# Half-width weight blocks, a later feed forward and loads on another queue in attention with a gated feed forward

## The chip, the cores and the metric

The kernel runs on one core of a Trainium2 chip. The core has TensorE (matrix products, called PE in the profile; its weight loads are PEld), VectorE (DVE), ScalarE (ACT), GpSimd (POOL) and SyncE (SP, which only issues transfers), and 16 DMA engines that all issuing queues share. The metric is the device time of one execution in microseconds.

## The reference

Eight batches of eight heads attend causally over 576 tokens with 64 columns a head, with a bias that falls with the running sum of `s`; the result, 4608 tokens by 512, goes through a gated feed forward of 1536 hidden columns.

```python
scores = scale * np.matmul(q, k.transpose(0, 1, 3, 2))
cum = np.cumsum(np.maximum(s, 0.0), axis=-1)
bias = -(cum[:, :, :, None] - cum[:, :, None, :])
scores = np.where(causal, -1000000000.0, scores + np.minimum(bias, 0.0))
attn = softmax(scores)                       # the largest score is subtracted first
x = concat_heads(np.matmul(attn, v))         # 4608 x 512
out = (sigmoid(x @ w_gate) * (x @ w_val)) @ w_out
```

Inputs are float32.

## The kernel before

**Precision.** Except for the first eight heads, which are computed in float32 (names with `n_`), operands are split into a high and a low float16 part, and a product is made of three: high by high, high by low, low by high.

**Tiles of a head.** The 576 queries of a head are five tiles: tile 0 has 64 rows, tiles 1 to 4 have 128. Tile t sees 64 + 128 t keys. Scores come from TensorE (`s_part`, lines 423 and 424); GpSimd masks the bias row (`mask_part`, 438); VectorE adds the bias and takes the extreme (`max_part`, 448); ScalarE takes the exponential into a float32 tile `e` (451). `p_part` then makes the float16 weights of several tiles at once, as `SETS` groups them: tiles 0 to 2 (768 columns) and tiles 3 and 4 (1152 columns). ScalarE writes the high part (455), VectorE the low part (456), and one DMA transpose on SP's queue (459) turns both into blocks of 128 keys by 128 queries, tile `pt`. A tile of 64 + 128 t keys is padded to t + 1 blocks, its last block half zeros; so a head has 15 high and 15 low blocks. `av_part` multiplies each of the 15 blocks of keys three times with the values (lines 471 to 473, tile `av`), and `x_part` divides by the sum of the weights, which is one more column of v.

**Values.** `load_v` (397 to 402) loads v for a pair of heads, `split_v` (409 to 412) splits it into `v16`. The power of two by which v is scaled is one for a batch: `v_square` (line 152) loads all v of the batch in four pieces of 288 KB into tiles `vsq`, through GpSimd's queue, into buffers that the bias rows `rl` use too (two of them); `v_square_sum` (160) squares and adds them on ScalarE; `v_scale` (164 on) adds over partitions. It is done one batch ahead: load at t = 2, square at t = 4 of heads 1 to 4 of the batch before.

**Keys and queries.** `split_qk` splits and transposes them into `T`; `swap_k` copies the halves of `T` crosswise (`T<-T`, lines 383 and 384). From head 18 on (`EARLY`), `more_room` gives the space of `t2big`, which only the feed forward of the first two token groups needs, to more buffers (`spare`; `t2f` in the profile).

**The bias row.** `load_crow` fetches a row of `cum_d` (389); `spread_crow` broadcasts it over the partitions on GpSimd (392).

**Feed forward.** Tokens are 18 groups of 256. A unit is a group and a block of 128 of the 1536 hidden columns: `ffn_in` (24 matmuls, line 619; 48 where a group lies across two batches), a tanh on ScalarE (624), VectorE (626), a split (634, 635), and `ffn_out`, which follows some units later (649), and after the last block ScalarE's `osb` (656) and the store on GpSimd's queue (657). The operand x sits in ten slots `xslots` (`x_of`), four to a batch, filled through a DMA transpose (`x<-x`, 491).

**What sets the order.** One loop over ticks n writes everything out; head i and tile 4 - t of it have tick n = 5 i + t. `p_part` of head a comes at ticks 5 a + 3 and 5 a + 6, `av_part` of head i - 2 at t = 1 of head i. A batch's feed forward is spread over the 40 ticks of the next batch, `m` ticks behind. From this order of writing as priority, the framework works out, with modelled durations, the order on each engine's queue, which is then fixed; `tc.high_priority` moves work ahead, `tc.keep_in_program_order` (`pin`, from head 18 on) keeps an instruction at its place in the written order. On the chip each queue runs strictly in its order.

Of the kernel before, what the change touches and what calls it, by code (L numbers as in the profile page):

```python
# [7 lines left out]
F16 = mybir.dt.float16  # L8
F32 = mybir.dt.float32
# [3 lines left out]
AF = mybir.ActivationFunctionType  # L13
# [3 lines left out]
P = 128  # L17
# [6 lines left out]
def tile_attention_then_gated_ffn(  # L24
# [27 lines left out]
    PAD = NTL * P - S  # L52
    NN = H
    LAG = 3

# [17 lines left out]
    e_s = [cp.tile([P, n * P], F32, name=f"e_{i}") for i, (_, _, n) in enumerate(SETS)]  # L73
    p_s = [cp.tile([P, 2, n * P], F16, name=f"p16_{i}") for i, (_, _, n) in enumerate(SETS)]
    e_t, pf_t = {}, {}
    for i, (ts, first_block, n) in enumerate(SETS):
        for t, kb in zip(ts, first_block):
            cols = slice(kb * P, (kb + t + 1) * P)
            e_t[t] = e_s[i][:, cols]
            pf_t[t] = p_s[i].rearrange("p l n -> p (l n)").bitcast(F32)[:, cols]  # L80
    for t, (q0, m, w) in enumerate(TILES):
        nc.gpsimd.memset(e_t[t][:, w:], 0.0)
# [28 lines left out]
    def pin(ins):  # L111

        return tc.keep_in_program_order(ins) if spare else ins
# [34 lines left out]
    def v_square(b, c):  # L148
        if c == 0:
            vss[b] = wp.tile([P, vch], F32, tag="vss", name=f"vss{b}")  # L150
        t = wp.tile([P, S], F32, tag="rl", name=f"vsq{b}_{c}")
        nc.gpsimd.dma_start(t, vview[b, c])
        if b == 0:
            nc.scalar.activation(t, t, AF.Square, accum_out=vss[b][:, c : c + 1])
        else:
            vsq[b, c] = t

    def v_square_sum(b, c):
        t = vsq.pop((b, c))
        pin(nc.scalar.activation(t, t, AF.Square, accum_out=vss[b][:, c : c + 1]))  # L160
# [158 lines left out]

    qk32, qkc, T, crow, v32, v16, PT, xq, S_ps, rl, AV = {}, {}, {}, {}, {}, {}, {}, {}, {}, {}, {}  # L320
    NG = (NT + GT - 1) // GT
# [69 lines left out]
    def spread_crow(i):  # L391
        pin(nc.gpsimd.partition_broadcast(crow[i], crow[i][0:1] if i > 0 else rel[0:1]))

# [11 lines left out]
    def split_v(p):  # L405

        sc = sv[2 * p // H][0]
        t = wp.tile([P, 5, 2, 2 * D + 2], F16, tag="v16", name=f"v16_{p}")
        nc.gpsimd.memset(t[:, :, :, 2 * D :], 1.0)
        src = v32[p][:, :, :, 0:D]  # L410
        nc.scalar.activation(t[:, :, :, D : 2 * D], src, AF.Copy, scale=sc)
        nc.vector.scalar_tensor_tensor(t[:, :, :, 0:D], src, sc, t[:, :, :, D : 2 * D], ALU.mult, ALU.subtract)
        v16[p] = t

    def s_part(i, t):
# [26 lines left out]
    def max_part(i, t):  # L442
        w = TILES[t][2]
        c = qkc[i // 2][1][:, 2:3]
        init = MASKED
        for n, (ps, a, b_) in enumerate(S_ps.pop((i, t))):
            acc = wp.tile([P, 1], F32, tag=f"em{n}", name=f"em{i}_{t}_{n}", bufs=3)
            nc.vector.tensor_tensor_reduce(e_t[t][:, a:b_], ps[:, : b_ - a], rl[i][:, a:b_], c, init,  # L448
                                           ALU.add, ALU.min, acc)
            init = acc  # L450
        nc.scalar.activation(e_t[t][:, :w], e_t[t][:, :w], AF.Exp, bias=init, scale=-1.0)  # L451

    def p_part(i, h_):

        nc.scalar.activation(p_s[h_][:, 0], e_s[h_], AF.Copy, scale=PSCALE)  # L455
        nc.vector.scalar_tensor_tensor(p_s[h_][:, 1], e_s[h_], PSCALE, p_s[h_][:, 0], ALU.mult, ALU.subtract)  # L456
        n = SETS[h_][2]
        PT[i, h_] = wp.tile([P, 2 * n, P], F16, tag=f"pt{h_}", name=f"pt{h_}_{i}")
        nc.sync.dma_start_transpose(PT[i, h_], p_s[h_].rearrange("p l n -> p (l n)"))

    def av_part(i, h_):
        p, j = divmod(i, 2)
        if i not in AV:
            AV[i] = pp.tile([P, NTL, D + 1], F32, tag="av", name=f"av{i}", bufs=1)
        pt = PT.pop((i, h_))
        ts, first_block, n = SETS[h_]
# [219 lines left out]
    FPT = 1.5  # L686
    EARLY = 18
    WLA = 3
    nticks = NTL * NH
    for n in range(nticks + 12):  # L690
# [48 lines left out]
        if i < NH:  # L739
            p, j = divmod(i, 2)  # L740
            b, h = divmod(i, H)
            if t == 0 and i + 1 < NH:
                load_crow(i + 1)
            if t == (2 if spare else 0) and i + 1 < NH:
                spread_crow(i + 1)
# [66 lines left out]
            if b + 1 < B:  # L812
                if t == 2 and 1 <= h < 1 + vch:
                    v_square(b + 1, h - 1)
                if t == 4 and 1 <= h < 1 + vch:
                    v_square_sum(b + 1, h - 1)
                if t == 1 and h == 6:
                    v_scale(b + 1)
            while n < NE and wnext["step"] < min(2 + n // 8, 6):
# [62 lines left out]
```

## Time and profile before

| | us |
|---|---|
| three runs | 1175.47, 1163.1, 1166.33 (median 1166.33) |
| the profiled execution | 1169.9 |
| its span, first to last instruction | 1168.0 |
| TensorE busy | 1106.7 (95%) |
| VectorE, ScalarE busy | 777.6 (67%), 753.6 (65%) |
| GpSimd busy | 307.5 (26%) |
| granted TensorE clock, mean | 0.975 |

In rows of groups stand: line, engine, operation, tile written and read, shapes, count, busy time in us and mean ns of one, and the idle time of the engine just before them with what ended it. A row of a timeline starts with the start and the duration in us. A row of stretches names the stretch, its length, then for each engine busy time and count, the granted clock, the DMA engines' busy share and GB/s. A wait list gives the waiter, what it waited for, the total in us, how often, and the longest.

### The profile page before, as it was taken

What the parts mean: (1) busy time and instruction counts of PE and PEld (TensorE: products, weight loads), DVE (VectorE), ACT (ScalarE), POOL (GpSimd) and SP (SyncE); (2) the same over time, 40 slices, a digit from 0 to 9 for tenths busy, and PEclk for the clock granted to TensorE, in tenths of its full rate; (3) what the DMA queues carried; (4) which work ended last, traced back from release to release, by engine and by line L of the source; (5) the groups of instructions that cost most, each with busy time, mean ns of one, the idle gap of its engine ahead of it and who ended that gap; (6) DMA issues with size and microseconds to landing.
All of it is one profiled execution on the core that took longest, in us unless ns stands there. A gap on an engine that the chain in (4) does not pass through costs nothing.

```text
span 1168.0 us, 30508 instructions
## 1 busy us (share of the span) xinstructions
PE 1106.7 (95%) x11924; PEld 868.5 (74%) x11924; DVE 777.6 (67%) x2113; ACT 753.6 (65%) x1465; POOL 307.5 (26%) x599
## 2 busy tenths in 40 slices
PE   6787599989999999999999999999999999999997
PEld 4666478757877887788777777778877887787774
DVE  6888789775887777766656578777777775222221
ACT  6979687675776777776646577767776765233222
POOL 5535433221233332222211132223222221000000
PEclk9878889999999999999999999999999999999999
DMA  9674988996999987875647577888977765000000
GB/s 274 198 217 116 177 162 177 167 179 139 168 148 179 172 166 149 161 156 116 122 87 145 125 138 164 147 168 163 162 156 147 129 116 105 19 20 20 1 19 19
DMA packets 464078, 157.49 MB, mean 135 GB/s; under 512 B 438399, under 2 KB 457855, under 8 KB 463934
## 3 DMA queue, kind: packets, MB, share of 16 engines
q1 hardware_dynamic: 446302, 119.89, 55.6%
q0 software_dynamic: 5440, 18.88, 5.6%
q10 hardware_dynamic: 12192, 16.78, 4.7%
q8 instruction: 93, 1.52, 0.5%
q14 instruction: 51, 0.42, 0.1%
HBM read 56.92 MB, written 9.58 MB: 57 GB/s over the span
## 4 chain that ended last, share of the span: by engine, by line
PE 59%; issue 23%; ACT 5%; DMA 5%; DVE 4%; POOL 3%; SPq 1%; ACTq 0%; POOLq 0%; DVEq 0%
PE gv L619 30%; PE o L649 16%; PE s L424 3%; PE s L423 2%; PE av L473 2%; PE av L471 2%; PE av L472 2%; DMA vsq<-in_v_dram 1%; PE na_ps L567 1%; DVE e L448 1%; PE s L537 1%; POOL rl L438 1%; DMA nqk<-in_q_dram 1%; DMA x<-x 1%; DMA T<-T 1%
## 5 line engine op out<-in xcount | busy, mean ns | idle before, releaser
L619 PE MATMUL gv<-x,w 128*128 128x256 f16 (+3 forms) x6912 | 614.1, 246 | 2.0 <-DMA x<-x 0.7
L619 PEld LDWEIGHTS <-w 128*128 128x128 f16 x6912 | 537.1, 98 | 61.1 <-issue 2.9
L649 PE MATMUL o<-w2all,h 128*128 128x512 f16 x1296 | 315.8, 379 | 3.2 <-ACT osb L656 3.2
L438 POOL TENSOR_SCALAR_AFFINE_SELECT rl<-rl 128x64 f32<-128x64 f32 (+1 forms) x280 | 132.2, 473 | 426.1 <-DVE em L448 365.9
L624 ACT ACTIVATE th<-gv,scb 128x256 f32<-128x256 f32 (+3 forms) x288 | 111.9, 414 | 193.1 <-PE gv L619 192.7
L649 PEld LDWEIGHTS <-h 128*128 128x128 f16 x1296 | 123.0, 98 | 107.2 <-issue 3.3
L451 ACT ACTIVATE e<-e,em 128x576 f32<-128x576 f32 x280 | 154.5, 556 | 67.8 <-DVE em L448 64.2
L626 DVE SCALAR_TENSOR_TENSOR t<-th,gv 128x256 f32<-128x256 f32 x192 | 80.2, 418 | 161.0 <-ACT th L624 160.6
L448 DVE CUSTOM_DVE_ANT_0 e<-s,rl,qkcf 128x288 f32<-128x288 f32 x280 | 134.4, 486 | 44.5 <-PE s L424 25.3
L456 DVE SCALAR_TENSOR_TENSOR p<-e,p 128x1152 f16<-128x1152 f32 x112 | 130.9, 1169 | 30.4 <-ACT p L455 29.7
L634 ACT ACTIVATE h<-t,hsc 128x256 f16<-128x256 f32 x192 | 97.0, 505 | 77.3 <-DVE t L626 77.3
L635 DVE SCALAR_TENSOR_TENSOR h<-t,hsc,h 128x256 f16<-128x256 f32 x192 | 92.5, 482 | 45.3 <-ACT h L634 44.9
L455 ACT ACTIVATE p<-e 128x1152 f16<-128x1152 f32 x112 | 111.8, 998 | 2.2
L471 PE MATMUL av<-v,pt 128*128 128x65 f16 x840 | 85.6, 193 | 10.9 <-DMA pt<-p 10.7
L471 PEld LDWEIGHTS <-pt 128*128 128x128 f16 x840 | 77.7, 98 | 18.0 <-DMA pt<-p 12.7
L472 PE MATMUL av<-v,pt 128*128 128x64 f16 x840 | 85.3, 193 | 0.0
L473 PE MATMUL av<-v,pt 128*128 128x65 f16 x840 | 85.1, 194 | 0.0
L472 PEld LDWEIGHTS <-pt 128*128 128x128 f16 x840 | 77.5, 97 | 5.2
L473 PEld LDWEIGHTS <-pt 128*128 128x128 f16 x840 | 77.5, 97 | 1.7 <-issue 0.8
L657 POOL DMA_DIRECT2D out_dram<-osb x36 | 20.3, 563 | 213.4 <-ACT osb L656 211.7
L423 PE MATMUL s<-T 128*128 128x288 f16 (+2 forms) x246 | 64.7, 278 | 5.5 <-DVE em L448 4.9
L424 PE MATMUL s<-T 128*128 128x288 f16 (+2 forms) x246 | 64.4, 278 | 4.1 <-DMA T<-T 4.1
(151 smaller groups left out, 1273.4 us busy)
## 6 DMA issues: line engine op xcount, KB each, us to landing
vsq<-in_v_dram POOLq DMA_DIRECT2D x32, 288.0 KB, 4.7
out_dram<-osb POOLq DMA_DIRECT2D x36, 256.0 KB, 2.6
v<-in_v_dram SPq DMA_DIRECT2D x64, 128.0 KB
T<-T SPq DMA_DIRECT2D x82, 72.0 KB
qk<-in_q_dram SPq DMA_DIRECT2D x17, 288.0 KB
qk<-in_k_dram SPq DMA_DIRECT2D x17, 288.0 KB
ws<-in_moe_w_out_dram ACTq DMA_DIRECT2D x4, 1024.0 KB
w2all<-in_moe_w_gate_dram ACTq DMA_DIRECT2D x7, 512.0 KB
```

The lines of the kernel that those rows point to most:

```text
L424: nc.tensor.matmul(ps[:, : b_ - a], lhs, T[i][:, 2, a:b_], start=False, stop=True)
L438: nc.gpsimd.affine_select(rl[i][:, q0:w], rl[i][:, q0:w], pattern=[[-1, m]], compare_op=ALU.is_ge, fill=-MASKED if i < NN else MASKED, bas ...
L448: nc.vector.tensor_tensor_reduce(e_t[t][:, a:b_], ps[:, : b_ - a], rl[i][:, a:b_], c, init, ALU.add, ALU.min, acc)
L451: nc.scalar.activation(e_t[t][:, :w], e_t[t][:, :w], AF.Exp, bias=init, scale=-1.0)
L455: nc.scalar.activation(p_s[h_][:, 0], e_s[h_], AF.Copy, scale=PSCALE)
L456: nc.vector.scalar_tensor_tensor(p_s[h_][:, 1], e_s[h_], PSCALE, p_s[h_][:, 0], ALU.mult, ALU.subtract)
L471: nc.tensor.matmul(AV[i][:, t], hi, v_[:, D : 2 * D + 1], start=kb == 0, stop=False)
L472: nc.tensor.matmul(AV[i][:, t, 0:D], hi, v_[:, 0:D], start=False, stop=False)
L473: nc.tensor.matmul(AV[i][:, t], lo, v_[:, D : 2 * D + 1], start=False, stop=kb == t)
L619: nc.tensor.matmul(ps[:, gv, a:e], w1[f][:, cc, gv, wl], x_of(b, cc)[:, xl, c0 + a : c0 + e], start=(c == 0), stop=(c == 3 * NC - 1))
L624: nc.scalar.activation(th[:, a:e], ps[:, 0, a:e], AF.Tanh, scale=scb[b][:, f : f + 1])
L649: nc.tensor.matmul(ps[:m], h[:, hl, tt * P : tt * P + m], w2[f][:, wl], start=(f == 0 and c == 0), stop=(f == NF - 1 and c == 2))
```

## The change

Four things change.

- **Half blocks, heads 18 to 63.** The columns of `e` are no longer padded: tile t takes 2 t + 1 half blocks of 64. In the float16 tile, a tile t has its t full high blocks, then one block made of the last high half and the last low half, then its t full low blocks: 2 t + 1 whole blocks, 25 a head. `p_halves` makes them with five ScalarE and seven VectorE instructions a head and transposes 9 and 16 blocks. `av_halves` multiplies full blocks as before and the mixed block with `vx`, in which the first 64 rows of every block of v stand twice, once with the high part's columns and once with the low part's. `split_v` fills `vx` with two transfers on SP's queue for each pair.
- **Loads of v for the scale.** From batch 2 on they are issued by SP. Batch 2's go into x slots at ticks 65 to 68 and are squared at 70 to 73, the last loaded first; later ones go into two buffers of `spare` at t = 0 of heads 2 to 5 and are squared at t = 4.
- **Feed forward.** From tick 111 on, `m` is n - 12 in place of n - 9.
- **Broadcast of the bias row.** At t = 2 from head 8 on (before: from head 18 on), in written order from row 9 on.

```diff
-    for name, n in (("qk16", QC * 2 * D), ("qk32", 4 * QC * D), ("T", 3 * S // 2)):
+    for name, n in (("qk16", QC * 2 * D), ("qk32", 4 * QC * D), ("T", 3 * S // 2), ("vsq0", S), ("vsq1", S),
+                    ("vx0", 5 * (2 * D + 2)), ("vx1", 5 * (2 * D + 2))):
 ...
-        t = wp.tile([P, S], F32, tag="rl", name=f"vsq{b}_{c}")
-        nc.gpsimd.dma_start(t, vview[b, c])
+        if b < 2:
+            t = wp.tile([P, S], F32, tag="rl", name=f"vsq{b}_{c}")
+        elif b == 2:
+            t = xslots[NX - 1 - c].rearrange("p l n -> p (l n)").bitcast(F32)[:, :S]
+        else:
+            t = spare[f"vsq{c % 2}"]
+        (nc.gpsimd if b < 2 else nc.sync).dma_start(t, vview[b, c])
 ...
+        spread = nc.gpsimd.partition_broadcast(crow[i], crow[i][0:1] if i > 0 else rel[0:1])
+        if i > NN:
+            tc.keep_in_program_order(spread)
 ...
         v16[p] = t
+        if spare:
+            x = spare[f"vx{p % 2}"].bitcast(F16).rearrange("p (c h n) -> p c h n", c=5, h=2)
+            for g in range(2):
+                nc.sync.dma_start(x[64 * g : 64 * g + 64], t[:64])
+            vx[p] = x
 ...
+    def p_halves(i, h_):
+        for t, _, _ in HALVES[h_]:
+            nc.scalar.activation(p_h[t][:, : (2 * t + 1) * 64], e_h[t], AF.Copy, scale=PSCALE)
+        for t, _, _ in HALVES[h_]:
+            if t:
+                nc.vector.scalar_tensor_tensor(p_h[t][:, (2 * t + 2) * 64 :], e_h[t][:, : t * P], PSCALE,
+                                               p_h[t][:, : t * P], ALU.mult, ALU.subtract)
 ...
+        for at in ((0, 1), (2,))[: 2 - h_]:
 ...
+            nc.vector.scalar_tensor_tensor(p_[:, ul], e_[:, ue], PSCALE, p_[:, uh], ALU.mult, ALU.subtract)
 ...
+    def av_halves(i, h_):
 ...
+            for kb in range(t):
+                v_ = v16[p][:, kb, j]
+                hi, lo = pt[:, b0 + kb], pt[:, b0 + t + 1 + kb]
+                nc.tensor.matmul(AV[i][:, t], hi, v_[:, D : 2 * D + 1], start=kb == 0, stop=False)
+                nc.tensor.matmul(AV[i][:, t, 0:D], hi, v_[:, 0:D], start=False, stop=False)
+                nc.tensor.matmul(AV[i][:, t], lo, v_[:, D : 2 * D + 1], start=False, stop=False)
+            v_ = vx[p][:, t, j]
+            nc.tensor.matmul(AV[i][:, t], pt[:, b0 + t], v_[:, D : 2 * D + 1], start=t == 0, stop=False)
+            nc.tensor.matmul(AV[i][:, t, 0:D], pt[:, b0 + t], v_[:, 0:D], start=False, stop=True)
 ...
-            if t == (2 if spare else 0) and i + 1 < NH:
+            if t == (2 if i >= NN else 0) and i + 1 < NH:
                 spread_crow(i + 1)
 ...
-        m = n - (9 if n > 2 * NTL * H + 30 else 7)
+        m = n - (LATE if n > 2 * NTL * H + 30 else 7)
```

More of the change, by code (lines that the diff above doesn't have):

```diff
@@ L53, in tile_attention_then_gated_ffn @@
     NN = H
+    EARLY = 18
     LAG = 3
@@ L74, in tile_attention_then_gated_ffn @@
     p_s = [cp.tile([P, 2, n * P], F16, name=f"p16_{i}") for i, (_, _, n) in enumerate(SETS)]
+    HALVES = ((((2, 0, 0), (1, 5, 10), (0, 8, 16))), ((4, 0, 0), (3, 9, 18)))
+    e_h, p_h = {}, {}
     e_t, pf_t = {}, {}
@@ L80, in tile_attention_then_gated_ffn @@
             pf_t[t] = p_s[i].rearrange("p l n -> p (l n)").bitcast(F32)[:, cols]
+        flat = p_s[i].rearrange("p l n -> p (l n)")
+        for t, ue, up in HALVES[i]:
+            e_h[t] = e_s[i][:, ue * 64 : (ue + 2 * t + 1) * 64]
+            p_h[t] = flat[:, up * 64 : (up + 4 * t + 2) * 64]
     for t, (q0, m, w) in enumerate(TILES):
@@ L317, in ffn_scale @@
             out_scale(b)
[L320 removed]
+    qk32, qkc, T, crow, v32, v16, vx, PT, xq, S_ps, rl, AV = {}, {}, {}, {}, {}, {}, {}, {}, {}, {}, {}, {}
     NG = (NT + GT - 1) // GT
@@ L443, in max_part @@
         w = TILES[t][2]
+        e_ = e_h if i >= EARLY else e_t
         c = qkc[i // 2][1][:, 2:3]
@@ L447, in max_part @@
             acc = wp.tile([P, 1], F32, tag=f"em{n}", name=f"em{i}_{t}_{n}", bufs=3)
-            nc.vector.tensor_tensor_reduce(e_t[t][:, a:b_], ps[:, : b_ - a], rl[i][:, a:b_], c, init,
+            nc.vector.tensor_tensor_reduce(e_[t][:, a:b_], ps[:, : b_ - a], rl[i][:, a:b_], c, init,
                                            ALU.add, ALU.min, acc)
             init = acc
-        nc.scalar.activation(e_t[t][:, :w], e_t[t][:, :w], AF.Exp, bias=init, scale=-1.0)
+        nc.scalar.activation(e_[t][:, :w], e_[t][:, :w], AF.Exp, bias=init, scale=-1.0)
     def p_part(i, h_):
+        if i >= EARLY:
+            return p_halves(i, h_)
         nc.scalar.activation(p_s[h_][:, 0], e_s[h_], AF.Copy, scale=PSCALE)
@@ L459, in p_part @@
         nc.sync.dma_start_transpose(PT[i, h_], p_s[h_].rearrange("p l n -> p (l n)"))
+    def p_halves(i, h_):
[5 more added lines that the diff above has]
+                                               p_h[t][:, : t * P], ALU.mult, ALU.subtract)
+        e_, p_ = (x[h_].rearrange(r, n=64) for x, r in ((e_s, "p (u n) -> p u n"), (p_s, "p l (u n) -> p (l u) n")))
+        for at in ((0, 1), (2,))[: 2 - h_]:
+            ue = [HALVES[h_][x][1] + 2 * HALVES[h_][x][0] for x in at]
+            up = [HALVES[h_][x][2] + 2 * HALVES[h_][x][0] for x in at]
+            ue, uh, ul = (slice(u[0], u[-1] + 1, max(u[-1] - u[0], 1)) for u in (ue, up, [u + 1 for u in up]))
+            nc.vector.scalar_tensor_tensor(p_[:, ul], e_[:, ue], PSCALE, p_[:, uh], ALU.mult, ALU.subtract)
+        n = sum(2 * t + 1 for t, _, _ in HALVES[h_])
+        PT[i, h_] = wp.tile([P, 2 * SETS[h_][2], P], F16, tag=f"pt{h_}", name=f"pt{h_}_{i}")
+        nc.sync.dma_start_transpose(PT[i, h_][:, :n], p_s[h_].rearrange("p l n -> p (l n)")[:, : n * P])
+    def av_halves(i, h_):
+        p, j = divmod(i, 2)
+        pt = PT.pop((i, h_))
+        for t, _, up in HALVES[h_]:
+            b0 = up // 2
+            for kb in range(t):
[7 more added lines that the diff above has]
+            nc.tensor.matmul(AV[i][:, t, 0:D], pt[:, b0 + t], v_[:, 0:D], start=False, stop=True)
     def av_part(i, h_):
@@ L464, in av_part @@
             AV[i] = pp.tile([P, NTL, D + 1], F32, tag="av", name=f"av{i}", bufs=1)
+        if i >= EARLY:
+            return av_halves(i, h_)
         pt = PT.pop((i, h_))
@@ L686, in tile_attention_then_gated_ffn @@
     FPT = 1.5
-    EARLY = 18
+    LATE = 12
+    VSQ = 65
     WLA = 3
@@ L811, in tile_attention_then_gated_ffn @@
                     v_scale(0)
-            if b + 1 < B:
+            if b == 0:
                 if t == 2 and 1 <= h < 1 + vch:
-                    v_square(b + 1, h - 1)
+                    v_square(1, h - 1)
                 if t == 4 and 1 <= h < 1 + vch:
-                    v_square_sum(b + 1, h - 1)
+                    v_square_sum(1, h - 1)
                 if t == 1 and h == 6:
+                    v_scale(1)
+            elif b == 1:
+                if VSQ <= n < VSQ + vch:
+                    v_square(2, n - VSQ)
+                if VSQ + 5 <= n < VSQ + 5 + vch:
+                    c = VSQ + 4 + vch - n
+                    v_square_sum(2, c)
+                if n == VSQ + 11:
+                    v_scale(2)
+            elif b + 1 < B:
+                if t == 0 and 2 <= h < 2 + vch:
+                    v_square(b + 1, h - 2)
+                if t == 4 and 2 <= h < 2 + vch:
+                    v_square_sum(b + 1, h - 2)
+                if t == 4 and h == 2 + vch:
                     v_scale(b + 1)
```

1 line of the change is left out of this document (removed).

## The prediction

> **What bounds the kernel now.** I read the page's head first, then the busy time of each engine by stretch of the span, then TensorE's groups in the long middle stretch, then the chain of waits, and last the single waits ahead of 350 us.
>
> ```profile
> span 1168.0 us, 30508 instructions
> PE 1106.7 (95%) x11924; PEld 868.5 (74%) x11924; DVE 777.6 (67%) x2113; ACT 753.6 (65%) x1465; POOL 307.5 (26%) x599
> ```
>
> ```profile
> core 0: us, PE busy (x) PEld busy (x) DVE busy (x) ACT busy (x) POOL busy (x), PEclk, DMA share, GB/s
> 0.00:150.00 150.00, 108.74 (x641) 85.75 (x642) 119.50 (x303) 119.44 (x224) 73.61 (x135) 0.83 0.75 194
> 150.00:240.00 90.00, 83.99 (x903) 68.83 (x901) 77.80 (x219) 64.88 (x123) 30.95 (x55) 0.98 0.87 172
> 240.00:350.00 110.00, 105.04 (x1278) 78.24 (x1276) 80.03 (x229) 80.37 (x164) 31.12 (x64) 1.00 0.87 157
> 350.00:1000.00 650.00, 649.27 (x7587) 513.82 (x7585) 462.43 (x1281) 441.96 (x856) 167.49 (x338) 1.00 0.74 143
> 1000.00:1152.00 152.00, 152.00 (x1481) 117.53 (x1480) 36.48 (x81) 44.53 (x98) 3.28 (x6) 1.00 0.04 14
> ```
>
> The stretches differ. From 350 to 1152 us TensorE (PE) is busy for 801.3 of 802 us at full clock, while VectorE (DVE) and ScalarE (ACT) are at 71% and 68% up to 1000 us. There, only TensorE's own work counts. Ahead of 350 us TensorE stands idle for 41 us in the first 150, and for 6 and 5 us in the next two stretches; there a wait can be worth something. A busy TensorE isn't yet one at its peak, so I looked at what it waits for in the long stretch and at the distance between two starts.
>
> ```profile
> L619 PE MATMUL gv<-x,w 128*128 128x256 f16 (+3 forms) x5636 | 491.1, 245 | 0.7 <-DMA x<-x 0.7
> L649 PE MATMUL o<-w2all,h 128*128 128x512 f16 x1044 | 255.9, 379 | 0.0
> L471 PE MATMUL av<-v,pt 128*128 128x65 f16 x630 | 61.7, 192 | 0.0
> ```
>
> ```profile
> 875.45 0.19 PE L471 MATMUL av<-v,pt 128*128 128x65 f16 x1
> ...
> 876.81 0.30 PE L423 MATMUL s<-t2f 128*128 128x320 f16 x1
> ...
> 949.02 0.10 PEld L473 LDWEIGHTS <-pt 128*128 128x128 f16 x1
> ```
>
> The first fence is the group list for 350 to 1150 us: of TensorE's groups these three show all the idle time there is in 800 us, 0.7 (the 630 of line 471 are 42 heads). The second is the order of time around one head's product of weights and values (a weight load from a later head beside it). A matmul of 65 columns is shown as 0.19 us long, but the next one starts long before that: the 45 of this head start from 875.45 on and the next work starts at 876.81, so one costs 1.36/45 = 0.0302 us. That, not 0.19, is what a removed matmul gives back.
>
> **The change part by part.**
>
> *Half blocks.* Today a head multiplies 15 key blocks three times, 45 matmuls. With the change a query tile t has t full blocks, three times each, and one mixed block (64 high and 64 low weights) that is multiplied twice: 3x(0+1+2+3+4) + 2x5 = 40. It holds for heads 18 to 63.
>
> ```profile
> 0.00:306.30 306.30, 17.44 (x150) 14.37 (x150) 0.91 0.80 179
> 306.30:1010.00 703.70, 67.70 (x690) 63.15 (x690) 1.00 0.75 142
> ```
>
> These are the matmuls of line 473 alone, 15 to a head: 150 of them are the ten heads 8 to 17, and the 690 after 306.3 us are the 46 heads the change touches. So the whole removal falls where TensorE is (all but) always busy: 46 x 5 x 0.0302 = **6.95 us less**. A weight load takes 0.10 us in the row at 949.02, more than three times the pitch, yet the starts don't wait for it. The Trainium skill ("TensorE: Matmul & The Clock Gate", section "LDWEIGHTS (loading the stationary operand)") gives a load as its columns divided by 1.2, some 107 ns for 128 columns, and its section on the issue gap has the spacing set by both operations; by that, the estimate is 230 x 0.107 = 24.6 us. The pitch of 0.03 us speaks against it.
>
> The same part changes the making of the weights:
>
> ```profile
> L456 DVE SCALAR_TENSOR_TENSOR p<-e,p 128x1152 f16<-128x1152 f32 x56 | 76.2, 1361 | 19.0 <-ACT p L455 18.6
> L455 ACT ACTIVATE p<-e 128x1152 f16<-128x1152 f32 x56 | 64.7, 1155 | 0.7
> L456 DVE SCALAR_TENSOR_TENSOR p<-e,p 128x768 f16<-128x768 f32 x56 | 54.7, 978 | 11.4 <-ACT p L455 11.1
> L455 ACT ACTIVATE p<-e 128x768 f16<-128x768 f32 x56 | 47.1, 841 | 1.5
> L459 SPq DMA_TRANSPOSE pt<-p x112: 1273/2545/4880, 129.2 to 990.7; - x112
> ```
>
> From the two sizes, ScalarE costs 0.818 ns a column and 213 ns an instruction, VectorE 0.997 and 212. Columns fall from 1920 to 1600 a head; instructions rise from 2 to 5 on ScalarE and from 2 to 7 on VectorE. ScalarE goes from 1996 to 5x213 + 1309 = 2374 ns (+0.38 us a head), VectorE from 2339 to 7x212 + 1595 = 3079 ns (+0.74). With some 42 heads in 350 to 1000 us that lifts VectorE from 462 to 493 us of 650 (76%) and ScalarE from 442 to 458 (70%): hidden under TensorE, priced at nothing. If that cover were gone, it would be 46 x 0.74 = 34 us. The transposes shrink from 30 to 25 blocks of 32 KB: 164 KB less a head, and a sixth of two issues of 2.545 us, 0.85 us less on SyncE's (SP's) queue.
>
> *Copies of v for the mixed block.* Per pair, two transfers of 64 partitions x 2600 bytes: 166 KB a head, which eats what the transposes save. On SP's queue they wait for VectorE's split of v; behind them stand the other head's transposes and the copies `T<-T`.
>
> ```profile
> 433.68 0.59 SPq L384 DMA_DIRECT2D T<-T  x1
> ...
> SPq L401 <- DVE v L412: 67.0, 20, 7.9
> ```
>
> By the row of a copy of 64 partitions an issue is 0.59 us, so one per head adds 0.6 us where 0.85 were saved. The second row is of SP's own wait list (total, times, longest): SP today already stands for that VectorE line 20 times, 67 us in all, and TensorE's idle of 0.7 us above shows that nothing comes of it. I take zero; the bound is in the rivals.
>
> *Loads of v for the scale.*
>
> ```profile
> vsq<-in_v_dram POOLq DMA_DIRECT2D x32, 288.0 KB, 4.7
> 256.44 0.68 ACT L160 ACTIVATE vsq<-vsq 128x576 f32<-128x576 f32 x1 [4.40 <-DMA vsq<-in_v_dram]
> 257.84 0.38 PE L649 MATMUL o<-w2all,h 128*128 128x512 f16 x1 [3.18 <-ACT osb L656]
> 145.77 0.68 ACT L160 ACTIVATE vsq<-vsq 128x576 f32<-128x576 f32 x1 [6.06 <-DMA vsq<-in_v_dram]
> 145.79 0.23 PE L471 MATMUL av<-v,pt 128*128 128x65 f16 x1 [8.02 <-DMA pt<-p]
> DVE rl L432 <- ACT vsq L160: 15.8, 13, 5.4
> POOL cr L392 <- DMA cr<-cum_d: 15.9, 9, 5.5
> L424 PE MATMUL s<-T 128*128 128x288 f16 (+4 forms) x33 | 8.4, 274 | 0.9 <-DMA T<-T 0.9
> 129.00:146.00 17.00, 6.16 (x50) 4.35 (x49) 11.75 (x36) 9.54 (x18) 4.01 (x9) 0.82 1.19 184
> ```
>
> 24 of the 32 loads move from GpSimd's queue to SP's, into room of their own, with four ticks from load to square instead of two for batches 3 to 7. At 252 us ScalarE stands 4.40 us for such a load and TensorE 3.18 us behind it: that goes, **3.2 us less**, and what is late next is a copy `T<-T`, 0.9 us in 240 to 350 us by the row of line 424. At 140 us ScalarE stands 6.06 us for batch 2's first load while TensorE waits 8.02 us for a transpose. That load leaves the place (batch 2's now start at tick 65); but TensorE's wait is named for another transfer, so between 0 and 8 us go. The load is 0.29 MB of some 3 MB (184 GB/s for 17 us) moved then, a tenth, and those engines are full (the last row): I take **1.5 us less**. New: batch 2's last load comes two ticks ahead of its square at tick 70, where a tick lasts 703.7/230 = 3.06 us by the later heads and a landing 4.7. That is a ScalarE stall of 0 to 6.06 us, hidden in part by the feed forward's two PSUM buffers: **1.5 us more**, a third of the shorter stall above. VectorE's waits for a buffer that the squares held (15.8 us) go beside other work: nothing. On SP four issues of 0.59 us in eight heads are 0.3 us a head, so 0.59 + 0.30 come where 0.85 go: nothing again. The Trainium skill ("DMA: Bandwidth & Descriptors", section "Issuing engines are not separate DMA queues") says that transfers from all queues share the same engines and another issuer saves only issue time; by it the move itself gives nothing. The trace agrees so far that the 3.2 us above come from distance in time and buffers, not from the queue.
>
> *Feed forward 12 ticks behind.* From tick 111 on, units are written out three ticks later. It may end the 0.7 us of waits for `x<-x` (**0.7 us less**). At tick 111 the pause in new units grows by three ticks, two units:
>
> ```profile
> 349.84 2.62 PE gv L619 x24
> ...
> 483.56 1.30 PE o L649 x6
> ...
> 300.00:350.00 50.00, 49.14 (x645) 39.28 (x642) 41.43 (x126) 38.16 (x79) 16.89 (x32) 1.00 0.98 167
> ```
>
> A unit is 2.62 + 1.30 us of TensorE, so at most 7.8 us lie bare; the present pause (7 to 9 ticks) falls in this stretch, whose idle time is 0.86 us in all. I take **0.5 us more**. After the last scores two more units remain, moved and not added.
>
> *Broadcasts of the bias row* move from tick 0 to tick 2 of heads 8 to 17, still three ticks ahead of use. GpSimd stands 15.9 us in all for such a row to land, the masks behind it on its queue with it (the row of line 392 above); with two ticks between, much of that goes, but beside other work: zero, and by the longest of these stands between 5.5 us less and 5.5 more.
>
> Sum: -6.95 - 3.2 - 1.5 + 1.5 - 0.7 + 0.5 = **-10.4 us**. The profiled execution took 1169.9 us (1.9 outside its span), so 1159.5 beside it; it lies 0.3% above the median of the runs, 1166.33, and beside that the forecast is **1156 us**, -0.9%.
>
> **The rivals.**
> 1. *Only the matmuls count*: a wait at batch 2's squares, the copies `T<-T` or the pause gives back the small gains. For it: SP's transfers share a DMA system at 0.87 there. 1166.3 - 7 = 1159. Chance 0.22.
> 2. *The early stage gains as a whole*: the 8.02 us go too, since ScalarE's 6.06 us end in the same moment. -6.95 - 3.2 - 0.7 - 8.0 = -18.9: 1147. Chance 0.17.
> 3. *Weight loads pace the short matmuls*: 230 x 0.10 (the row at 949.02) = 23, with the small gains 1166.3 - 23 - 3.4 = 1140. Against it stands the pitch. Chance 0.03. It is the rule of the Trainium skill weighed above ("TensorE: Matmul & The Clock Gate", "LDWEIGHTS (loading the stationary operand)").
> 4. *The pause at tick 111 lies bare*: +7.3 on the forecast, 1163. Chance 0.06.
> 5. *Slower: SP's queue.* A pair's copies of v wait for VectorE at the head of SP's queue and hold the next `T<-T` past its scores. A stand is 67.0/20 = 3.35 us; were a third of it bare on TensorE in each of 23 pairs, 26 us more, 1182; it ends over 1% slower from (10.4 + 11.7)/23 = 0.96 us a pair on. Against it: today's 67 us of such stands leave TensorE 0.7 us of idle. Chance 0.08.
>
> **How the numbers follow.** The forecast has 0.44. About 1% (11.7 us) is what a measurement here can tell from no change. Faster by more means under 1154.7: rivals 2 and 3 nearly whole (0.19) and some 0.2 of the forecast's 0.44, which sits 1.3 us above that line: 0.39. Slower: rival 5 and a little: 0.09. The rest, 0.52, lies within 1%. The range 1145 to 1166 leaves out rivals 3 and 5 and the tails; the forecast's own is 1150 to 1161.
>
> **What would show it.** Right: 40 matmuls a head at a pitch of 0.03 us, idle under 1 us in TensorE's groups from 350 us on, the last feed forward ending some 10 us earlier, no ScalarE stand of over 3 us for `vsq`, VectorE near 76% in the long stretch. Wrong: TensorE idle behind `T<-T`, `vx` or the transposes after 306 us; idle around 330 us (the pause); a new ScalarE stand near 205 us; or idle ahead of 150 us that changes by more than 8 us, since the planned order may differ there.

## The result

The changed kernel is slower, by 0.7%: its time is 1178.32 us against 1170.75 us for the kernel before (20 runs of each, medians, 7.6 us apart). Over all these runs the ratio is 1.0071, with a 95% interval of 1.0045 to 1.0097. The forecast was 1156 us, in a range of 1145 to 1166. The profiled execution took 1172.0 us, the shortest of its 20, so the profile below shows only 2.2 us of the 7.6 that were lost; a ratio counts for more here than a span.

The head of the page after, and the busy time by stretch, with the same bounds as before:

```profile
span 1170.2 us, 30499 instructions
PE 1100.7 (94%) x11694; PEld 860.9 (74%) x11694; DVE 784.6 (67%) x2343; ACT 756.3 (65%) x1603; POOL 282.4 (24%) x575
```

```profile
0.00:150.00 150.00, 115.64 (x709) 91.03 (x710) 125.90 (x318) 122.65 (x229) 74.59 (x137) 0.85 0.73 202
150.00:240.00 90.00, 70.85 (x781) 58.62 (x779) 66.91 (x192) 59.58 (x111) 29.07 (x45) 0.92 0.88 147
240.00:350.00 110.00, 105.16 (x1243) 77.95 (x1242) 79.60 (x246) 76.79 (x172) 29.10 (x57) 1.00 0.82 162
350.00:1000.00 650.00, 645.39 (x7416) 508.74 (x7416) 473.35 (x1504) 449.11 (x990) 145.29 (x329) 1.00 0.75 144
```

230 matmuls are gone, as they should be, and TensorE's busy time is 6.0 us less. Its idle time is more: in the first 150 us 34.4 us instead of 41.3, then 19.2 instead of 6.0, 4.8 instead of 5.0, and from 350 to 1000 us 4.6 instead of 0.7. That is 10.0 us more over the four stretches, lost at two places: between 150 and 240 us, and just behind 350 us. What the first stretch shows as won can't be relied on: the run with 9 ticks below, whose TensorE has the same order of work up to 345 us, stands idle there for 45.4 us. From 350 to 1000 us VectorE's share is 73%, ScalarE's 69%: neither looks like a bound.

The first place, from the order of time of the changed kernel (start, duration, what; in brackets the idle time before it):

```profile
170.01 3.23 SPq L484 DMA_TRANSPOSE pt<-p  x1
170.61 0.44 ACTq L258 DMA_DIRECT2D ws<-in_moe_w_out_dram  x1
...
181.05 8.73 SPq L484 DMA_TRANSPOSE pt<-p  x1
189.36 0.10 PEld L531 LDWEIGHTS <-pt 128*128 128x128 f16 x1 [13.26 <-DMA pt<-p]
...
189.40 1.16 ACT L480 ACTIVATE p<-e 128x1152 f16<-128x1152 f32 x1 [12.24 <-DMA pt<-p]
```

A transpose of weights issued at 170.01 us lands at 189.3; the chain of waits has it as one piece of 19.3 us. TensorE stands 13 us for it, and ScalarE 12.2. 0.6 us behind the transpose, ScalarE had issued a load of `w_out`: 1 MB, since the feed forward's weights lie in memory with 64 bits an element (the section on the reference calls all inputs float32, which is wrong for these). The stretches of 4 us from 172 us on show what the DMA engines did with the two:

```profile
172.00:176.00 4.00, 4.00 (x37) 3.35 (x35) 2.93 (x9) 3.43 (x8) 1.83 (x3) 1.00 1.32 153
176.00:180.00 4.00, 0.38 (x4) 0.10 (x1) 2.55 (x7) 1.15 (x2) 2.06 (x4) 1.00 1.42 83
180.00:184.00 4.00, 0.00 (x0) 0.00 (x0) 0.00 (x0) 0.00 (x0) 0.00 (x0) 0.59 1.07 71
184.00:188.00 4.00, 0.00 (x0) 0.00 (x0) 0.00 (x0) 0.00 (x0) 0.00 (x0) 0.50 1.44 191
188.00:192.00 4.00, 2.64 (x35) 2.44 (x36) 1.41 (x2) 2.20 (x2) 0.00 (x0) 0.50 0.66 139
```

The last two columns are the engines' busy share and GB/s: over 1.0 of busy time, and 71 to 83 GB/s moved at the worst. Every compute engine stands. The packets themselves became slow: on SP's queue 6836 packets of 270 bytes on average took 23 ns each from 164 to 174 us, and 912 packets of 250 bytes took 139 ns each from 174 to 184 us. The third column from the end is the granted clock: 1.00 when the stand begins at 176 us, 0.59 on average from 180 to 184 us, and 0.50 from there until work has resumed. The Trainium skill ("TensorE: Matmul & The Clock Gate", section "Part 1: The HAM clock gate") puts the half clock behind an idle window of about 3.4 us; this stand, 4 us old when the clock is still 1.00 and halved before it is 8 us old, agrees.

The second place, from the groups of TensorE between 300 and 1000 us:

```profile
L445 PE MATMUL s<-T 128*128 128x320 f16 (+1 forms) x177 | 46.1, 277 | 2.7 <-DVE em L471 2.7
L445 PE MATMUL s<-t2f 128*128 128x288 f16 (+2 forms) x90 | 24.0, 277 | 3.8 <-DVE em L471 2.6 <-DMA t2f<-qk 1.2
```

Scores wait for a PSUM buffer that VectorE's bias step (`em`) still reads. Before, the same two stages stood for 0.9 us in all (a copy `t2f<-t2f`). TensorE is in front of VectorE there; it ought to have units of the feed forward to do meanwhile.

### The profile page after: what moved, and what is told of

It reads as the page before. It is cut to its first block, busy times and chain, and to the rows that moved or that the text cites. A ratio compares the mean times of both kernels' runs of the same rounds, so it can differ in the third digit from the quotient of the medians.

```text
span 1170.2 us, 30499 instructions
## 1 busy us (share of the span) xinstructions
PE 1100.7 (94%) x11694; PEld 860.9 (74%) x11694; DVE 784.6 (67%) x2343; ACT 756.3 (65%) x1603; POOL 282.4 (24%) x575
## 4 chain that ended last, share of the span: by engine, by line
PE 56%; issue 21%; DMA 7%; DVE 6%; ACT 5%; POOL 2%; SPq 2%; POOLq 0%; ACTq 0%; DVEq 0%
PE gv L679 29%; PE o L709 15%; DMA pt<-p 3%; PE s L446 3%; PE s L445 2%; DMA T<-T 1%; PE na_ps L627 1%; DVE e L471 1%; PE av L514 1%; PE av L512 1%; PE av L513 1%; DMA T<-qk 1%; POOL rl L460 1%; DVE p L481 1%; POOL cr L460 1%
## 5 line engine op out<-in xcount | busy, mean ns | idle before, releaser
L460 POOL TENSOR_SCALAR_AFFINE_SELECT rl<-rl 128x64 f32<-128x64 f32 (+1 forms) x280 | 129.2, 462 | 510.7 <-DVE em L471 462.0
L488 ACT ACTIVATE p<-e 128x576 f16<-128x576 f32 (+4 forms) x230 | 106.0, 463 | 15.1 <-DMA pt<-p 11.4
L491 DVE SCALAR_TENSOR_TENSOR p<-e,p 128x512 f16<-128x512 f32 (+3 forms) x184 | 90.0, 489 | 36.7 <-ACT p L488 35.7
L407 POOL PARTITION_BROADCAST cr<-cr x63 | 59.3, 941 | 1.8 <-DMA cr<-cum_d 1.7
L454 DVE TENSOR_SCALAR rl<-cr,qkcf 128x576 f32<-128x576 f32 x56 | 29.1, 519 | 42.5 <-POOL cr L407 42.4
L513 PE MATMUL av<-v,pt 128*128 128x64 f16 x460 | 55.2, 192 | 0.0
L514 PE MATMUL av<-v,pt 128*128 128x65 f16 x460 | 55.1, 194 | 0.0
L512 PE MATMUL av<-v,pt 128*128 128x65 f16 x460 | 55.1, 193 | 0.0
L513 PEld LDWEIGHTS <-pt 128*128 128x128 f16 x460 | 43.1, 97 | 4.6
```

Source lines behind the costliest of these rows:

```text
L460: nc.gpsimd.affine_select(rl[i][:, q0:w], rl[i][:, q0:w], pattern=[[-1, m]], compare_op=ALU.is_ge, fill=-MASKED if i < NN else MASKED, bas ...
L488: nc.scalar.activation(p_h[t][:, : (2 * t + 1) * 64], e_h[t], AF.Copy, scale=PSCALE)
L491: nc.vector.scalar_tensor_tensor(p_h[t][:, (2 * t + 2) * 64 :], e_h[t][:, : t * P], PSCALE, p_h[t][:, : t * P], ALU.mult, ALU.subtract)
L513: nc.tensor.matmul(AV[i][:, t, 0:D], hi, v_[:, 0:D], start=False, stop=False)
```

## The experiments

All ratios are to the kernel before, with 95% intervals. The base is the changed kernel, unless it is said to be the kernel before. Each edit can also change the order that the framework plans, and where that matters it is said.

### One part alone, or one part undone

**Half blocks alone** (feed forward 9 ticks behind, broadcasts and loads of v as before, these with their ticks and tiles):

```diff
-    LATE = 12
+    LATE = 9
 ...
-        (nc.gpsimd if b < 2 else nc.sync).dma_start(t, vview[b, c])
+        nc.gpsimd.dma_start(t, vview[b, c])
 ...
-            if t == (2 if i >= NN else 0) and i + 1 < NH:
+            if t == (2 if spare else 0) and i + 1 < NH:
 ...
```

> The change with only its half blocks (feed forward 9 ticks behind, loads of v through GpSimd as before, bias rows broadcast as before). The planned order of every engine is that of the kernel before up to the feed forward's start for batch 1, so the early stage is the same. Theory A (the half blocks give what the removed matmuls cost, and the change loses it in its other parts): 7 us less than the kernel before, ratio 0.994 (0.992 to 0.997). Rival B (the half blocks themselves cost: more instructions on ScalarE and VectorE, copies of v on SP's queue): no gain or a loss, ratio 0.999 or more, with TensorE idle after 306 us.

Measured: 1.0065 (1.0034 to 1.0097), span 1173.2 us. Seven microseconds of matmuls went and the kernel became slower. The order is that of before up to about tick 90 (TensorE's up to 273 us), so what is lost here is the half blocks' own.

```profile
L672 PE MATMUL gv<-x,w 128*128 128x256 f16 (+3 forms) x4791 | 411.1, 244 | 6.2 <-DMA x<-x 6.2
L438 PE MATMUL s<-T 128*128 128x320 f16 (+1 forms) x177 | 46.0, 277 | 0.8 <-DVE em L464 0.8
L438 PE MATMUL s<-t2f 128*128 128x288 f16 (+2 forms) x90 | 24.1, 277 | 1.7 <-DMA t2f<-qk 1.7
```

From 300 us on TensorE now stands 6.2 us for the operand x of the feed forward, at the starts of four batches, where the kernel before stood 0.7.

**The changed kernel with 9 ticks**, and **the kernel before with 12**:

```diff
-    LATE = 12
+    LATE = 9
```

> The change with the feed forward 9 ticks behind in place of 12; the planned order is that of the changed kernel up to about tick 111. The changed kernel has 5.5 us of idle TensorE between 349 and 392 us, just after the pause in new units. Theory A (the longer pause lies bare): that idle goes, some 4 to 5 us less than the changed kernel, ratio to the kernel before about 1.003. Rival (the idle comes from transfers and would be there without the pause): ratio stays at 1.007 and the idle stays.

Measured: 1.0123 (1.0073 to 1.0173). The waits for x come back (6.0 us by TensorE's groups).

```diff
-        m = n - (9 if n > 2 * NTL * H + 30 else 7)
+        m = n - (12 if n > 2 * NTL * H + 30 else 7)
```

> The kernel before with nothing changed but the feed forward, 12 ticks behind in place of 9 (planned order the same up to about tick 111). Theory C (the pause in new units lies bare on TensorE by itself, and the later feed forward only pays where something else delays x): TensorE gains some 3 to 5 us of idle between 330 and 400 us and loses the 1.1 us behind the transposes of x; 2 to 4 us more, ratio 1.002 to 1.004. Rival D (the pause is bare only because the half blocks make a head's work on ScalarE and VectorE longer): no new idle there, ratio 0.998 to 1.001.

Measured: 1.0004 (0.9968 to 1.004). So 12 ticks seem worth 0.5% where half blocks stand (1.0123 against 1.0071; the intervals overlap), and nothing where they don't. With the waits for x, 6.0 us with 9 ticks and none with 12, they mend what half blocks break.

**The changed kernel with the loads of v as before**, with their ticks and tiles:

```diff
-        (nc.gpsimd if b < 2 else nc.sync).dma_start(t, vview[b, c])
+        nc.gpsimd.dma_start(t, vview[b, c])
 ...
```

> The change with the loads of v for the scale as before (GpSimd's queue, buffers shared with the bias rows, batch 2's at heads 9 to 12). Theory A1 (moving those loads is what costs the early stage): the early loss of some 7 to 11 us goes, the pause's stays, ratio to before 0.997 to 1.000. Rival A2 (the later broadcast of the bias rows costs it): ratio stays at 1.005 to 1.008. Rival A3 (any other planned order of the early stage does, by where the last loads of w_out meet the transposes): no sign forecast, but then the idle before a head's first product of weights and values, behind a transpose under way during a w_out load, differs by 5 us or more.

Measured: 1.0092 (1.0058 to 1.0126). The new loads may be worth 0.2%, 2.5 us; the intervals overlap, so the size is open.

**The broadcast as before in the changed kernel, and the moved broadcast alone in the kernel before** (each with its place in the written order):

```diff
 ...
-            if t == (2 if i >= NN else 0) and i + 1 < NH:
+            if t == (2 if spare else 0) and i + 1 < NH:
```

> The change with the bias rows broadcast as before (tick 0 up to head 17, free order). Theory A2 (the later broadcast costs the early stage): ratio to before 0.997 to 1.000. Rival A1 (the move of the loads of v does): ratio stays at 1.005 to 1.008. Rival A3 (planned order against w_out's loads): no sign forecast; the idle behind a transpose during a w_out load tells.

Measured: 1.000 (0.996 to 1.004), span 1163.2 us.

```diff
 ...
-            if t == (2 if spare else 0) and i + 1 < NH:
+            if t == (2 if i >= NN else 0) and i + 1 < NH:
```

> The kernel before with nothing changed but the bias rows' broadcast (tick 2 from head 8 on, in written order). Theory A2 (it costs the early stage by itself): head 18's scores start 5 to 10 us later, ratio 1.004 to 1.009. Rival E (it costs only together with the moved loads of v or the half blocks): ratio 0.998 to 1.002.

Measured: 1.0057 (1.0023 to 1.0091). The part that I had priced at zero costs 0.6 to 0.7%, alone and with the rest. Of ten small instructions on an engine that is busy for a quarter of the time this can hardly be the work; the edit changes the planned order from about tick 40 on.

### Why the early stage lost

**All loads of w_out through SP**, then **through GpSimd**, in the changed kernel:

```diff
-            if n < 2:
+            if n < 2 or o:
                 nc.sync.dma_start(dst, src)
```

> The changed kernel with the six loads of w_out issued by SP in place of ScalarE, so that they stand in one queue with the transposes and don't run beside them. Theory H (a load of w_out beside transposes slows both to under 100 GB/s for some 10 us, and the changed order of the early stage meets it more often): no transpose of 10 us or more between 110 and 200 us, the 13 us of idle before a head's first product there go, ratio to before 0.997 to 1.001. Rival I (the early loss is not of that kind): ratio 1.005 or more; a load standing ahead of the transposes on SP could itself cost up to 5 us each.

Measured: 0.9958 (0.9931 to 0.9986).

```diff
-                d = nc.scalar.dma_start(dst, src)
+                d = (nc.gpsimd if o else nc.scalar).dma_start(dst, src)
```

> The changed kernel with the w_out loads issued by GpSimd instead of ScalarE. If what hurts is a large load on another queue beside SP's transposes: a gap of 8 to 13 us near 140 or 180 us stays, ratio 1.005 to 1.010. Rival (only the load's place in time mattered, and any other place relieves it): near 0.996, as with SP.

Measured: 0.9962 (0.9935 to 0.999), and no gap over 3.5 us at either place. So a second queue beside SP's need not hurt, and the theory that it always does has fallen. But both edits change the order of the whole early stage.

**Only the last of these loads through SP.** TensorE, VectorE and GpSimd then run their instructions in the same order as in the changed kernel. Of SP's, one other moves, which the expectation overlooks: a load of v of 32 KB, issued at 180.3 us in the changed kernel, comes two transposes later (187.7 us).

```diff
-                d = nc.scalar.dma_start(dst, src)
+                d = (nc.sync if n == len(wsteps) - 1 else nc.scalar).dma_start(dst, src)
```

> The changed kernel, only the last 1 MB load of w_out issued by SP instead of ScalarE; no other instruction changes its place in any queue. If this load beside the transposes causes TensorE's gap of 13.1 us at 176 us: the gap falls under 5 us, ratio 0.997 to 1.000. Rival (the order of the early stage costs it, the load is only beside it): a gap of 8 us or more stays there, ratio 1.005 or more.

Measured: 0.9988 (0.9957 to 1.002), 0.83% under the changed kernel, for one transfer of 1 MB. Its order of time at that place:

```profile
173.83 3.42 SPq L484 DMA_TRANSPOSE pt<-p  x1
177.34 0.54 SPq L258 DMA_DIRECT2D ws<-in_moe_w_out_dram  x1
...
180.45 0.20 PE L531 MATMUL av<-v,pt 128*128 128x65 f16 x1 [0.24 <-DMA pt<-p]
```

and one of its stretches of 4 us:

```profile
180.00:184.00 4.00, 3.76 (x56) 3.30 (x55) 4.00 (x8) 3.28 (x4) 2.48 (x3) 1.00 1.15 328
```

In SP's queue the load has to come behind the transpose, TensorE waits 0.24 us for the weights instead of 13, and from 180 to 184 us 328 GB/s are moved instead of 71. So the load of w_out at this place is the cause of the gap; the load of v can't have begun it, since in the changed kernel it is issued 10 us behind the transpose, when TensorE has stood for 4 us. With 0.83% the loss of the broadcast (0.7%) is accounted for.

**Only the last load through GpSimd** (the planned order changes a little behind it):

```diff
-                d = nc.scalar.dma_start(dst, src)
+                d = (nc.gpsimd if n == len(wsteps) - 1 else nc.scalar).dma_start(dst, src)
```

> The same load issued by GpSimd; here the planned order changes a little behind it. If what hurts is ScalarE's queue beside SP's: as with SP, 0.997 to 1.000. If any second queue beside SP's transposes hurts: gap of 8 us or more, 1.005 or more.

Measured: 1.0006 (0.9979 to 1.0033); a gap of 6.7 us stays at 180 us. That lies between the two expectations, so this run doesn't decide what about the two transfers makes them slow together.

**w_out through SP in the kernel before, and in the kernel before with the moved broadcast:**

```diff
-            if n < 2:
+            if n < 2 or o:
```

> The kernel before, with only the 1 MB loads of w_out issued by SP instead of ScalarE. Theory of the collision (a large load on ScalarE's queue running beside the transposes on SP's queue slows both): before has one such place, TensorE's gap of 8.2 us from 137.5 us on; it goes, ratio 0.993. Rival (the gain of the same edit in the changed kernel belongs to the order that the change made there): 1.000 here. A third (SP stands longer, so the transposes behind the load come late): 1.005.

Measured: 0.9995 (0.9967 to 1.0022). My expectation of 0.993 fell. TensorE's gap of 8.0 us at 138 us did go, but the scores of head 8 start 7.6 us later (120.3 us against 112.7), with loads of w_out now ahead of their transfers in SP's queue.

> The kernel before with the moved broadcast alone, and w_out issued by SP. The moved broadcast alone cost 0.57%. If it cost that through the collision of the w_out loads with the transposes: the same as the kernel before with w_out on SP, within 0.3%. Rival (it costs by the new order on GpSimd and VectorE itself, ahead of 350 us): 0.5 to 0.6% more than that kernel.

Measured: 0.9997 (0.9976 to 1.0018), the same as without the moved broadcast. With the loads out of the way, the broadcast costs nothing. So its price was where it put the work beside these loads.

### Why half blocks lost

**The copies of v for the mixed block through GpSimd**, with half blocks alone:

```diff
-                nc.sync.dma_start(x[64 * g : 64 * g + 64], t[:64])
+                nc.gpsimd.dma_start(x[64 * g : 64 * g + 64], t[:64])
```

> The half blocks alone as in the first experiment, but the copies of v for the mixed block issued by GpSimd in place of SP. Theory F (those copies stand at the head of SP's queue until VectorE has split v and hold the transposes of x behind them, so that the feed forward waits for x at each batch's start): TensorE's waits for x of 6.9 us (392, 512, 790 and 907 us) fall to about 1 us, and the time by 5 to 8 us: ratio to before 0.999 to 1.002 where the first experiment had 1.0065. Rival G (more work on ScalarE and VectorE delays x): the waits stay at 5 us or more and the ratio at 1.004 or more.

Measured: 1.0118 (1.0064 to 1.0172); the waits for x grow, to 10.6 us. So nothing speaks for these copies at the head of SP's queue holding x back (the place of my rival 5); the next run has the same waits without any such copy.

**The kernel before, weights made in pieces.** Whole blocks, all 45 matmuls, no `vx`; only more instructions for the weights of heads 18 to 63, two on ScalarE and three on VectorE for each set. This adds 0.40 us on ScalarE and 0.67 us on VectorE to a head, somewhat more than half blocks do (0.33 and 0.45):

```diff
-        nc.scalar.activation(p_s[h_][:, 0], e_s[h_], AF.Copy, scale=PSCALE)
-        nc.vector.scalar_tensor_tensor(p_s[h_][:, 1], e_s[h_], PSCALE, p_s[h_][:, 0], ALU.mult, ALU.subtract)
+        for r in pieces([n // 2]):
+            nc.scalar.activation(p_s[h_][:, 0, r], e_s[h_][:, r], AF.Copy, scale=PSCALE)
+        for r in pieces([n // 3, 2 * n // 3]):
+            nc.vector.scalar_tensor_tensor(p_s[h_][:, 1, r], e_s[h_][:, r], PSCALE, p_s[h_][:, 0, r], ALU.mult, ALU.subtract)
```

> The kernel before, its whole blocks kept, but from head 18 on the weights are made in pieces: four ScalarE instructions a head instead of two and six VectorE instructions instead of two (0.43 us and 0.85 us more a head, about what half blocks add). No matmul goes and no transfer changes. Theory (the longer ScalarE and VectorE work of a head is what TensorE waits for in half blocks alone): TensorE's idle time after 300 us grows from 6 to about 15 us, with waits for x at the starts of batches, ratio 1.008. Rival (the copies of v and the smaller transposes do it): idle stays at 6 us, 1.000.

Measured: 1.0126 (1.0085 to 1.0168), and the same waits as with half blocks alone, larger (the profile is of the slowest of its six runs, 1193.1 us; their median is 1183.28):

```profile
L624 PE MATMUL gv<-x,w 128*128 128x256 f16 (+3 forms) x4706 | 401.4, 244 | 8.4 <-DMA x<-x 8.2 <-DVE t L631 0.2
L423 PE MATMUL s<-T 128*128 128x320 f16 (+1 forms) x173 | 45.0, 277 | 2.2 <-DVE em L448 2.2
L423 PE MATMUL s<-t2f 128*128 128x288 f16 (+2 forms) x90 | 24.2, 277 | 4.2 <-DVE em L448 4.2
```

The longer making of the weights is enough for it, with no copy of v and no changed transpose. SP's queue around the start of a batch's feed forward shows how; first the kernel before, then half blocks alone, then the pieces:

```profile
383.03 2.77 SPq L459 DMA_TRANSPOSE pt<-p  x1
385.90 1.34 SPq L491 DMA_TRANSPOSE x<-x  x1
```

```profile
388.07 3.46 SPq L495 DMA_TRANSPOSE pt<-p  x1
391.58 2.10 SPq L544 DMA_TRANSPOSE x<-x  x1
...
395.71 3.04 PE L672 MATMUL gv<-x,w 128*128 128x128 f16 x27 [3.09 <-DMA x<-x]
```

```profile
388.71 2.79 SPq L464 DMA_TRANSPOSE pt<-p  x1
391.60 1.34 SPq L496 DMA_TRANSPOSE x<-x  x1
...
395.61 1.67 PE L624 MATMUL gv<-x,w 128*128 128x128 f16 x27 [1.73 <-DMA x<-x]
```

The transpose of x stands in SP's queue behind one of weights, and that one goes 5.0 and 5.7 us later than before; x follows it, 5.7 us later in both. This is not one late transpose. The transpose of x three pairs of heads earlier goes at 301.2 us before, at 302.6 with half blocks alone and at 303.9 with the pieces, so the three pairs take 84.7, 89.0 and 87.7 us: 4.3 and 3.0 of the 5.7 us are lost in them, and the rest earlier. Whether the longer instructions do this themselves, or the order that the framework plans from longer modelled ones, these runs don't separate.

**The same with 12 ticks:**

```diff
-        m = n - (9 if n > 2 * NTL * H + 30 else 7)
+        m = n - (12 if n > 2 * NTL * H + 30 else 7)
```

> The same with the feed forward 12 ticks behind. Theory: the waits for x go, and the pause of TensorE at tick 111 lies bare as in the changed kernel (4 to 5 us between 350 and 390 us, where the kernel before with 12 ticks alone has 1.4), ratio 1.004. Rival: the pause stays covered, 1.4 us, ratio 1.000.

Measured: 1.0063 (1.0032 to 1.0095).

```profile
L423 PE MATMUL s<-T 128*128 128x320 f16 (+1 forms) x177 | 46.0, 277 | 1.3 <-DVE em L448 1.3
L423 PE MATMUL s<-t2f 128*128 128x288 f16 (+2 forms) x90 | 24.0, 277 | 3.1 <-DVE em L448 3.1
L424 PE MATMUL s<-t2f 128*128 128x288 f16 (+2 forms) x90 | 23.4, 277 | 1.7 <-DMA t2f<-t2f 1.7
```

No wait for x is left, and the scores wait for VectorE as in the changed kernel. The kernel before with 12 ticks alone has 0.5 us of these waits for `em`. So the pause in new units at tick 111 lies bare when a head's work on VectorE and ScalarE is longer, and stays covered when it is not.

### A version that is faster than both

The old broadcast, w_out through SP, half blocks, loads of v and 12 ticks as in the change; then the same with the 12 ticks reached one at a time:

```diff
-            if n < 2:
+            if n < 2 or o:
 ...
-            if t == (2 if i >= NN else 0) and i + 1 < NH:
+            if t == (2 if spare else 0) and i + 1 < NH:
```

> Half blocks, loads of v on SP and 12 ticks, but the broadcast where it was, and w_out issued by SP. Theory of the collision: the kernel with the old broadcast has only gaps of 1.8 and 4.3 us at the w_out loads, and stood at 1.000; the ratio falls by at most those 6 us, 0.995. Rival (the edit is worth 1.1% wherever it is put, as in the changed kernel): 0.989. A third (the order is already good, SP only stands longer): 1.000 or more.

Measured: 0.9931 (0.9907 to 0.9954), 1160.77 us.

```diff
-        m = n - (LATE if n > 2 * NTL * H + 30 else 7)
+        m = n - min(LATE, max(7, 7 + (n - 2 * NTL * H - 30) // 10))
```

> As the run before it, and the feed forward's distance of 12 ticks is reached in single steps of one tick in every ten, instead of at once at tick 111. If the pause at tick 111 is what lies bare from 350 to 390 us (4.3 to 5.5 us with half blocks): most of it goes, 0.3 to 0.4% less than the run without the steps. Rival (ScalarE's and VectorE's longer work of a head is late there whatever the feed forward does): the same within 0.1%.

Measured: 0.9893 (0.9862 to 0.9923), **1156.31 us**, 1.1% faster than the kernel before. The pause was it: the step from one to the other is 0.38%, 4.5 us (nine runs from 1156.87 to 1163.64 us, then six from 1153.66 to 1159.29), and TensorE's busy time between 300 and 420 us rises from 113.20 to 116.91 us, 3.7 of these. First row without the steps, second with them:

```profile
300.00:420.00 120.00, 113.20 (x1402) 89.95 (x1400) 94.52 (x311) 86.60 (x197) 33.30 (x69) 1.00 0.91 169
```

```profile
300.00:420.00 120.00, 116.91 (x1468) 93.68 (x1466) 95.05 (x316) 89.00 (x200) 31.17 (x70) 1.00 0.89 169
```

## Why the prediction was wrong

**The removed matmuls: right.** 230 are gone, at the pitch that was taken:

```profile
610.00 0.19 PE L512 MATMUL av<-v,pt 128*128 128x65 f16 x1
...
611.18 0.19 PE L517 MATMUL av<-t2f,pt 128*128 128x64 f16 x1
611.21 2.78 PE L679 MATMUL gv<-x,w 128*128 128x256 f16 x24
```

The 40 matmuls of a head start within 1.21 us, 0.0302 each: 6.95 us for 230. The weight loads don't pace them. The figures of the Trainium skill ("TensorE: Matmul & The Clock Gate", sections "Back-to-back issue gap" and "LDWEIGHTS (loading the stationary operand)"), some 107 ns for a load of 128 columns, are met in length (0.10 us) but not as a spacing.

**ScalarE's and VectorE's instructions, priced at nothing: the first step that failed.** Their cost was right, rather high: with half blocks alone the instructions of a head sum to 2.32 us on ScalarE and 2.79 on VectorE, 0.33 and 0.45 us more, where 0.38 and 0.74 were forecast. The cover was wrong. I argued from 350 to 1000 us as a whole: TensorE always busy, VectorE at 76% (measured: 73%). But TensorE has something to do only while units of the feed forward are ready, and at a batch's start (9 ticks) or at the pause (12 ticks) it hasn't. There a head's chain of scores, bias, exponential, weights, transpose and x is the bound, whatever the share over 650 us. Taking the pieces as the price, which is rather high, since they add more to a head than half blocks do, this is 0.63% with 12 ticks, 7.4 us, all that the matmuls gave; its interval reaches from 3.7 to 11 us. The sums agree: the changed kernel with the old broadcast stands at 1.000, -7.0 + 7.4, and half blocks alone, with 9 ticks, at +7.6 us, -7.0 + 14.7 by the pieces with 9 ticks. That the longer work itself is the reason, and not the order planned with it, is not shown.

**The broadcasts, priced at zero, between 5.5 us less and 5.5 more: the second.** They cost 0.57% alone, 6.7 us, and 0.71% beside the other parts. I looked for the cost in GpSimd's waits. It came through the planned order, which put a transpose beside a load of 1 MB. The same thing stood in the profile before, and I read it as a full DMA system instead of a collapse. Here is its stretch around TensorE's 8.02 us, 93 GB/s at a busy share of 1.70:

```profile
134.00:138.00 4.00, 3.56 (x33) 2.97 (x32) 3.70 (x7) 4.00 (x7) 0.29 (x1) 1.00 1.70 93
```

With both, -7.0 + 7.4 + 6.7 = +7.1 us, the first from the pitch and the other two from runs of these parts; the whole change measured +8.3 (0.71% of 1170).

**The pause at tick 111: the mechanism was right, as rival 4, the size and the chance wrong.** I took 0.5 us, since the present pause cost nothing, and 0.06 for the case that it lies bare. It lies bare, with 5.3 us of idle TensorE from 349 to 392 us where the kernel before had none, and at 4.5 us by the run in single steps (part of the 7.4 us above), because the cover had been used up by the step above. The two edits were priced one by one, and they hide behind the same units.

**x<-x, 0.7 us less: right** for the edit with 12 ticks. No wait for x is left in the changed kernel after 300 us.

**The loads of v: right in kind.** ScalarE's stand of 4.4 us at 252 us is gone. The new one at batch 2's squares is 3.4 us in all, against a bound of 6.06; the row is of the list of waits:

```profile
ACT x L174 <- DMA x<-in_v_dram: 3.4, 4, 1.6
```

What this part gives in the end, 3.2 us by the sum, is some 2.5 us by the run that undoes it, and by the overlap of the intervals it may be nothing.

**Rival 5, SP's queue: wrong.** The kernel ended on its side, but the copies of v are not the reason. SP's wait for VectorE's split of v grew by little (70.7 us in all, 67.0 before), and with the copies moved away the waits for x grew.

**What remains open.** Why a transpose and a large load are so slow together at 176 us and not at other places where both run at once. With all loads through GpSimd, transposes ran beside them with no stand of over 3.5 us; with the last alone there, 6.7 us were left. And the profile after shows 2.2 us of the 7.6 us between the medians. The run with 9 ticks tells how the rest can arise: with the same early order as the changed kernel its profile has two stands for a transpose beside such loads, 8.6 us at 139 us and 12.2 us at 185 us, where the profile after has only the second. So the early stage differs from execution to execution; how often the changed kernel meets both, no run counts. The profile before has a stand at the first of these places too, so single profiles of this stage are to be compared with care.

## What to carry to other kernels

An engine at 75% is a cover only where the bounding engine has other work ready; check the starts of batches and every pause, not the mean of the stage, before pricing extra instructions at nothing. Edits that each lean on the same cover are to be priced together. Where a planner writes the queues, an edit of no work still moves large transfers, so look for what each large transfer runs beside; moving one such load to the queue of the transposes was worth more in the changed kernel than the 230 matmuls.

## What the hardware showed

A transpose beside one load of 1 MB took four times as long as the next of its kind that the end waited for. From the chain of waits of the changed kernel (start, length, what), the longest two of weights:

```profile
170.01 19.30 DMA pt<-p
...
318.45 4.91 DMA pt<-p
```

The DMA engines were busy throughout and moved 71 to 83 GB/s at the worst: a packet took 139 ns in place of 23 on SP's queue, and 510 ns on the queue of the load, where a packet has about 4 KB. With the load behind the transpose in SP's own queue, 328 GB/s were reached, and from 180 to 182 us, when nearly all packets were the load's, one took 164 ns. The Trainium skill ("DMA: Bandwidth & Descriptors", section "Issuing engines are not separate DMA queues") says that transfers of all issuers share the engines and interleave, and that another issuer saves only issue time. The trace agrees that they share: from 174 to 184 us SP's queue took 79% of the 16 engines' time and the load's queue 44%. It does not agree that only issue time is at stake: in SP's queue the same transfer has its place in an order, and that was worth 0.83% here.
